# Batched DMA transposes in a fused attention and wave-MLP kernel: q in one long transpose and a tail, batch 2 by TensorE

## The chip, the cores and the metric

The kernel runs on one core of one Trainium2 chip. The metric is the device time of one execution in microseconds; lower is better. Each kernel is executed many times, and the median stands for it. The profile records one further execution on the core: its span runs from the first to the last instruction, and the execution's own time includes what lies around the span.

The engines in the profile are PE (TensorE matmuls), PEld (TensorE weight loads), DVE (VectorE), ACT (ScalarE), POOL (GpSimd) and SP (SyncE, which here issues the DMAs of the main work). A trailing q, as in SPq, names an engine's sequencer.

## The reference

Eight batches of 576 tokens, 8 heads of 64. First a linear attention without softmax, with a norm per head; its output, heads side by side, is x of 576x512 per batch. Then a token mixer with phases and a channel mixer.

```
kv  = k^T v                      per head, 64x64
o   = q kv
x   = o / sqrt(mean(o*o) + 1e-6) * g_norm
theta = x @ w_theta              512x512
y   = w_tok_r @ (x * cos(theta)) + w_tok_i @ (x * sin(theta))      576x576 over tokens
u   = x + y
out = u + max(u @ w_ch, 0)       512x512
```

Inputs and output are float32. Inside, everything but kv is computed with float16 operands.

## The kernel before

Tokens of a batch are cut into four full tiles of 128 and a last one of 64 (`ti` or `j` from 0 to 4, `NF` = 4 full ones, `T` = 64). Heads are handled in four pairs `hp`, so that a pair fills 128 partitions; channels are cut into four chunks `kc`. A batch passes these stages:

- `load` brings q, k and v by head pair (12 transfers of 256 or 288 KB a batch) and the 64 last tokens in the tails kl, vl, ql of 128 KB. `cast_q` casts q on VectorE to float16 in `qcast`, of which there are two, used by even and odd batches.
- q has to lie with channels on partitions. For batches 0 and 1, `by_pair` does that with TensorE: four transposes of 128x128 a pair (`qTps`), copied from PSUM to `qT`, and `turn_q_tail` for the last 64 tokens. For batches 2 to 7, `turn_q` (L502 to L514) issues five DMA transposes from SyncE, one for each token tile, of 128x512 and 64x512, from `qcast` to `qT`.
- `attention` forms k^T v of a pair in PSUM (kv) and copies it to the block-diagonal `kvbd`. `norm` multiplies q with it (raw), squares on ScalarE (sq), sums per head on VectorE (ss), takes the power -1/2 on GpSimd (rt), and scales on VectorE (x).
- `turn_x` transposes x by TensorE (xTps) and scales it by g_norm on ScalarE (xT).
- `phase` forms theta (th), takes it to the range of the sine with pt (ScalarE), f and fa (VectorE), computes both sines on ScalarE (tr), and multiplies by x (z, VectorE).
- `mix` forms y transposed, over six pieces of a batch, and adds x on VectorE (uT).
- `channel` needs u with tokens on partitions: TensorE transposes uT (ups) and ScalarE copies it (u), except for batches 5 and 6 (`U_FROM` = 5), where DMA transposes of 256 columns bring it to `ub`, eight a batch. Then vps = u @ w_ch on TensorE, ot = max(vps, 0) + u on VectorE, and a store by SyncE.

`load_weights` brings w_theta (wst), both mixers (wmix) and w_ch (wcs) in chunks through a ring of 6 staging buffers (`wst` in `SLOTS`); each chunk is cast to float16 by whichever of ScalarE, VectorE or GpSimd the planner picks, which frees its buffer. `mixer_step` transposes the mixers with TensorE to `wT`. `idle_work` offers TensorE filler matmuls named `warm`.

Nothing runs in the order in which it is written here. Each step is added to `Weave` with the engines that could do it, a cost, a due time, what it needs, and the buffers it makes and uses. `Weave.run` goes through a planned time of its own and, for each engine, picks the step that can start soonest and is due first; then it writes the instructions down. The due times come from `DUE`: a first time and a step per item, shifted by `PERIOD` per batch. `MARGIN`, `SLACK`, `URGENT` and `WARM` set how the planner chooses. `in_traced_order` fixes the resulting order on each engine. At run time each engine takes its instructions in exactly this order, so one that waits holds back everything behind it on its engine. This holds for SyncE's DMA queue as well: a DMA whose semaphore is not there yet holds back all later ones, loads and stores alike. The planner itself gives at most 8 DMAs in flight (`LANES`).

```
SLOTS = {
    "kv": 1, "raw": 2, "tp": 2, "th": 1, "mm": 3,
    "k": 6, "v": 6, "q": 6, "ql": 1, "tails": 2, "qc": 2, "qT": 2, "bd": 2, "sq": 2, "ss": 6,
```

`SLOTS` says how many buffers of a kind there are; kv, raw, tp and mm are the eight PSUM banks, and mm serves th, y, vps and warm alike.

Of the kernel before, what the change touches and what calls it, by code (L numbers as in the profile page):

```python
# [18 lines left out]
PERIOD = 25.94  # L19
START = 4.0  # L20
DUE = {
    "load": (-10.17, 8.21),
    "theta": (6.75, 0),
    "mixers": (16.79, 2.63),
    "wch": (26.26, 6.01),
    "wT": (19.93, 1.18),
    ("phase", 0): (10.7, 0),
    ("mix", 0): (28.21, 4.45),
    ("channel", 0): (37.27, 8.33),
    ("phase", 1): (10.01, 3.64),  # L30
    ("mix", 1): (40.08, 5.47),
    ("channel", 1): (54.07, 9.91),
    ("first", 1): (-17.91, 0),
    "first": (-12.95, 0.43),
    "cast": (23.48, 1.17),
    "turn_q": (-8.79, 0),
    "attention": (-4.98, 1.92),
    "norm": (6.64, 1.4),
    "turn": (5.35, 1.03),
    "phase": (19.29, 3.62),  # L40
    "mix": (52.62, 3.55),
    "channel": (67.69, 3.8),
# [5 lines left out]
    "wst": 6, "z0": 2, "z1": 2, "z2": 2, "z3": 2, "z4": 2,  # L48
# [3 lines left out]
U_FROM = 5  # L52
X_FROM = 8
MIX_AFTER = 3
WCH_AFTER = 9


class Weave:
# [8 lines left out]
    SLACK = {"PE": 0.045, "ACT": 0.032, "DVE": 0, "POOL": 0.1, "SP": 0.05}  # L67
    MARGIN = {"PE": 0.282, "ACT": 0.015, "DVE": 0.624, "POOL": 0.1, "SP": 0.0}
    LANES = 8
    BEGIN = {"PE": 1.6, "ACT": 3.2, "DVE": 1.7, "POOL": 2.5, "SP": 0.73}  # L70
    WARM = 69.2
    COLD = 5.0
    URGENT = 2.7
# [20 lines left out]
    def run(self):  # L94
# [92 lines left out]
        assert all(t[0][0] == "warm" for t in ready) and not wanted  # L187
# [19 lines left out]
def kernel(  # L207
# [112 lines left out]
    def idle_work(n):  # L320
        name = f"warm{n}"

        def fn(e):
            t = ps("mm", [P, SH], FP32, name)
            nc.tensor.matmul(
                t[:], kv_bd[1][:, 0, :], kv_bd[1][:, 0:2, :].rearrange("p h c -> p (h c)"),
                start=True, stop=True,
            )

        weave.add(("warm", n), [("PE", 0.11, 0.2, False)], 1e6, fn, makes=[("mm", name)])  # L330

    def load(b, hp):
# [31 lines left out]
        for (i, (kind, src)) in enumerate((("q", q), ("k", k), ("v", v))):  # L364
            full = kind == "q" or b >= QUAD
            weave.add((kind, b, hp), [sp(0.47 if full else 0.42)], due("load", b, hp) + 0.01 * i, part(kind, src),
                      makes=[(kind, f"{kind}{b}_{hp}")], dma=dma(0.85 if b == 0 and hp < 2 else 0.73), load=True)
        if hp == (0 if b else HP - 1):
            for (i, (kind, src)) in enumerate((("kl", k), ("vl", v), ("ql", q))):
                if b < QUAD and kind != "ql":  # L370
                    continue
                weave.add((kind, b), [sp(0.64)], due("load", b, hp) + 0.04 + 0.01 * i,
# [4 lines left out]
                          dma=dma(1.1), load=True)  # L377
# [124 lines left out]
    def turn_q(b):  # L502
        for j in range(NT):
            def fn(e, j=j):
                if j == 0:
                    st["qT", b] = sb("qT", [P, HP, S], FP16, f"qT{b}")
                rows = P if j < NF else T
                nc.sync.dma_start_transpose(
                    out=st["qT", b][:, :, j * P:j * P + rows],
                    in_=qcast[b % 2][:rows, j].rearrange("p h d -> p (h d)"),  # L510
                )
            weave.add(("qT", b, j), [sp(1.3)], due("turn_q", b, j), fn,
                      needs=[("qc", b, hp) for hp in range(HP)] + [("qcl", b)],
                      makes=[] if j else [("qT", f"qT{b}")],  # L514
                      uses=[f"qc{b}"] + ([f"qT{b}"] if j else []),
                      dma=dma(1.05))

    def attention(b, hp):
        def fn(e):
# [3 lines left out]
            if b >= QUAD:  # L523
                for j in range(NT):
                    for r in range(2):
                        nc.tensor.matmul(  # L526
                            kvp[r * D:(r + 1) * D, hp, :],
                            st["k", b, hp][:, r, j, :] if j < NF
                            else st["kl", b][:, 2 * hp + r, :],
                            st["v", b, hp][:, r, j, :] if j < NF  # L530
                            else st["vl", b][:, 2 * hp + r, :],
                            start=(j == 0), stop=(j == NT - 1),
                        )
                return
            for j in range(NS):
                for r in range(2):
                    half = slice(r * PH, (r + 1) * PH)
                    nc.tensor.matmul(  # L538
                        kvp[r * D:(r + 1) * D, hp, :], st["k", b, hp][half, j, :],
                        st["v", b, hp][half, j, :], start=(j == 0), stop=(j == NS - 1),  # L540
                    )
# [19 lines left out]
    def norm(b, ti):  # L561
# [4 lines left out]
        def product(e):  # L566
            t = st[raw] = ps(bank, [P, C], FP32, raw)
            for hp in range(HP):
                qT = st["qT", b][:, hp, :]
                for (rows, cols) in (  # L570
                    ((slice(0, P), slice(ti * P, (ti + 1) * P)),) if ti < NF
                    else ((slice(0, T), slice(SF, S)), (slice(T, P), slice(SF, S)))
                ):
                    nc.tensor.matmul(  # L574
                        t[rows, hp * P:(hp + 1) * P], qT[:, cols], kv_bd[b % 2][:, hp, :],
# [39 lines left out]
        qTs = [("qT", b, i) for i in range(NT)]  # L615
# [14 lines left out]
    def by_pair(b, hp):  # L630

        raw, sq, ss, rt, px, pq = (f"{n}{b}h{hp}" for n in ("raw", "sq", "ss", "rt", "xTps", "qTps"))
        at = due("first", b, hp)
        home = "xT" if b else "uT"
        pair = slice(2 * hp, 2 * hp + 2)
        bank = "mm" if b == 0 and hp > 1 else "raw"
        (qTn, bdn, kvn, xn, xTn) = (f"{n}{b}" for n in ("qT", "bd", "kv", "xp", "xT"))
# [9 lines left out]
        def keep_q0(e):  # L647
            if hp == 0:
                st["qT", b] = sb("qT", [P, HP, S], FP16, qTn)
            t = st["qT", b][:, hp, 0:SF]  # L650
            if e == "ACT":
                nc.scalar.copy(out=t, in_=st[pq][:])
            else:
                nc.vector.tensor_copy(t, st[pq][:])
# [10 lines left out]
        def product(e):  # L665
            t = st[raw] = ps(bank, [P, NF, P], FP32, raw)
            for ti in range(NF):
                nc.tensor.matmul(
                    t[:, ti, :], st["qT", b][:, hp, ti * P:(ti + 1) * P], kv_bd[b % 2][:, hp, :],
# [51 lines left out]
        def keep(e):  # L721
# [6 lines left out]
            else:  # L728
# [5 lines left out]
        weave.add((pq,), [pe(0.25)], at, turn_q0, needs=[("qc", b, hp)], makes=[("tp", pq)],  # L734
                  uses=[f"qc{b}"])
        weave.add(("qT", b, hp), [act(SF), dve(0.35, True)], at, keep_q0, needs=[(pq,)],
                  makes=[] if hp else [("qT", qTn)], uses=[pq] + ([qTn] if hp else []))
# [20 lines left out]
    def turn_q_tail(b):  # L758
# [10 lines left out]
        def keep(e):  # L769
            t = st["qT", b][:, :, SF:S]  # L770
# [5 lines left out]
        at = due("first", b, HP - 1) - 0.1  # L776
# [5 lines left out]
    def turn_x(b, ti):  # L782
# [38 lines left out]
        if b >= X_FROM:  # L821
            weave.add(("xd", b, ti), [sp(1.3)], at, turn_by_dma, needs=[(f"x{b}_{ti}",)],
                      makes=[("xT", f"xT{b}")] if start else [],
                      uses=[f"x{b}_{ti}"] + ([] if start else [f"xT{b}"]), dma=dma(1.05))
# [148 lines left out]
    def channel(b, ti):  # L973
# [49 lines left out]
        def turn_by_dma(kc, half):  # L1023
            def fn(e):
                if not kc and not half:
                    st["ub", b] = sb("ub", [P, NF, C], FP16, f"ub{b}")
                nc.sync.dma_start_transpose(
                    out=st["ub", b][:, 2 * half:2 * half + 2, kc * P:(kc + 1) * P],
                    in_=st["uT", b][:, kc, half * SH:(half + 1) * SH],
# [9 lines left out]
        elif ti % 2 == 0:  # L1039
            for kc in range(NK):  # L1040
                weave.add(("ud", b, kc, ti // 2), [sp(0.8)], at - 2.0, turn_by_dma(kc, ti // 2),
                          needs=[("uT", b, 2 + kc if ti else kc // 2)],
# [72 lines left out]
```

## Time and profile before

| what | value |
|---|---|
| time, median of 11 runs | 230.75 us (227.09 to 233.35) |
| the profiled execution's own time | 231.21 us |
| its span | 229.4 us |
| granted TensorE clock | 1.0 |
| PE, DVE, ACT, POOL busy | 92%, 78%, 68%, 35% of the span |
| HBM read, written | 33.06 MB, 9.44 MB |
| q transposes by DMA | 30, median 3.6 us from issue to landing |
| u transposes by DMA | 16, median 2.3 us |

Busy times are sums over one execution. Matmuls are pipelined, and the end of one is modelled, so a busy TensorE may still hold stops: its rate is read from the starts of matmuls that follow each other. In lists of waits a line reads: engine and line that waited, what ended the wait, then total us, number and the longest. In the chain in order of time a line gives its start, its length and what held the chain then. In a timeline of SyncE a line gives start and length, the latter from the first issue to the end of the last of a merged group; the number after x counts instructions. In a tile's view three numbers with slashes are the shortest, median and longest duration in ns. DMA share is the mean busy share of the core's 16 DMA engines.

The loads are spread over most of the span: the last v of batch 7 lands at 162.0 us. The last matmul starts at about 225 us, and the last store lands at 228.4.

### The profile page before, as it was taken

The page shows a single profiled execution, that of the slowest core. Times are in us where ns is not written, and L with a number is a line of the kernel's source. Part 1 is how long each engine was busy: PE and PEld are TensorE (multiplying, and loading weights), DVE is VectorE, ACT ScalarE, POOL GpSimd, SP SyncE. Part 2 cuts the span into 40 slices and gives each one's busy share as a digit, 9 for nine tenths or more (in the row PEclk, how much of TensorE's full clock was granted, in tenths as well). Part 3 has the DMA queues.
Part 4 walks back from the last instruction along what each step waited for, and adds up shares of the span by engine and source line. Part 5 has one row for each costly group of instructions (what it writes and reads, how often), then busy time and mean ns, then how long its engine had stood idle before and what let it go on. Part 6 is the DMA issues. An engine that isn't in the chain of part 4 may idle for free.

```text
span 229.4 us, 5990 instructions
## 1 busy us (share of the span) xinstructions
PE 211.2 (92%) x2354; PEld 144.6 (63%) x2354; DVE 179.6 (78%) x359; ACT 156.0 (68%) x303; POOL 81.1 (35%) x94
## 2 busy tenths in 40 slices
PE   6779979999977999799988989999999999999992
PEld 4666568874656666575666656567657666657661
DVE  2177798695966699988887879998999898986552
ACT  3378989683990789767867678797788766663031
POOL 6024304660006533560264507532654065500000
PEclk9999999999999999999999999999999999999999
DMA  6999999999759978999699699999532323323414
GB/s 198 376 304 292 281 338 281 239 359 229 143 155 311 296 94 209 352 291 102 201 292 266 150 330 311 248 159 272 147 88 83 83 57 116 106 57 92 163 46 160
DMA packets 62399, 47.47 MB, mean 207 GB/s; under 512 B 32548, under 2 KB 54052, under 8 KB 62372
## 3 DMA queue, kind: packets, MB, share of 16 engines
q1 hardware_dynamic: 62368, 47.11, 77.9%
q8 instruction: 18, 0.29, 0.6%
q14 instruction: 9, 0.07, 0.1%
q10 hardware_dynamic: 4, 0.00, 0.0%
HBM read 33.06 MB, written 9.44 MB: 185 GB/s over the span
## 4 chain that ended last, share of the span: by engine, by line
PE 56%; DMA 25%; DVE 9%; SPq 3%; ACT 2%; issue 2%; POOL 1%; DVEq 0%; POOLq 0%
PE y L940 23%; PE vps L998 10%; DMA q<-in_q_dram 8%; PE th L844 7%; DMA k<-in_k_dram 6%; DMA v<-in_v_dram 5%; DMA wst<-in_moe_w_theta_dram 3%; PE kv L526 3%; PE raw L574 3%; DVE f L860 2%; PE xTps L791 2%; PE kv L538 2%; DMA wmix<-in_moe_w_tok_r_dram 2%; PE ups L989 2%; SPq L339 1%
## 5 line engine op out<-in xcount | busy, mean ns | idle before, releaser
L940 PE MATMUL y<-wT,z 128*128 128x320 f16 (+1 forms) x576 | 77.9, 286 | 0.8 <-DVE f L860 0.8
L940 PEld LDWEIGHTS <-z 128*128 128x128 f16 x576 | 54.5, 98 | 16.9 <-issue 1.6
L596 POOL TENSOR_TENSOR rt<-ss,mhalf 128x8 f32<-128x8 f32 x31 | 53.3, 1720 | 2.6
L592 POOL TENSOR_SCALAR ss<-ss 128x8 f32<-128x8 f32 x31 | 9.6, 308 | 85.4 <-DVE ss L585 84.7
L998 PE MATMUL vps<-wch,uT 128*128 128x512 f16 (+1 forms) x192 | 37.2, 344 | 0.0
L951 DVE SCALAR_TENSOR_TENSOR uT<-y,gcol,xT 128x320 f16<-128x320 f32 (+1 forms) x48 | 29.3, 611 | 6.5 <-PE y L940 6.3
L844 PE MATMUL th<-wth,xT 128*128 128x512 f16 x128 | 32.3, 380 | 0.7 <-DVE f L860 0.5
L856 ACT ACTIVATE pt<-th,magic_t 128x512 f32<-128x512 f32 (+1 forms) x40 | 25.5, 641 | 8.6 <-PE th L844 5.5
L800 ACT ACTIVATE xT<-xTps,gcol 128x512 f16<-128x512 f16 (+1 forms) x32 | 20.1, 632 | 13.5 <-PE xTps L791 12.9
L860 DVE SCALAR_TENSOR_TENSOR f<-pt,th 128x512 f32<-128x512 f32 (+1 forms) x40 | 24.9, 627 | 4.1 <-ACT pt L856 4.0
L879 ACT ACTIVATE tr<-f 128x512 f16<-128x512 f32 x32 | 19.9, 628 | 11.1 <-DVE f L860 11.0
L484 DVE CAST qcast<-q 128x512 f16<-128x512 f32 x32 | 13.7, 432 | 16.0 <-DMA q<-in_q_dram 15.0
L1005 ACT COPY u<-ups 128x512 f16<-128x512 f16 (+1 forms) x32 | 16.4, 526 | 13.8 <-PE ups L989 13.6
L879 ACT ACTIVATE tr<-fa,pio_t 128x512 f16<-128x512 f32 x32 | 22.9, 720 | 2.0 <-DVE fa L867 1.7
L608 DVE TENSOR_TENSOR x<-raw,rt 128x512 f16<-128x512 f32 x32 | 21.9, 684 | 1.5 <-POOL rt L596 1.1
L585 DVE TENSOR_REDUCE ss<-sq 128x8 f32<-128x512 f32 x32 | 21.5, 677 | 1.9 <-ACT sq L581 1.8
L1009 DVE SCALAR_TENSOR_TENSOR ot<-vps,u 128x512 f32<-128x512 f32 (+1 forms) x32 | 19.5, 616 | 3.2 <-PE vps L998 2.0
L897 DVE TENSOR_TENSOR z<-x,tr 128x1024 f16<-128x1024 f16 (+1 forms) x32 | 19.7, 616 | 1.5 <-ACT tr L887 1.4
L998 PEld LDWEIGHTS <-uT 128*128 128x128 f16 (+1 forms) x192 | 14.4, 102 | 9.8 <-issue 0.8
L581 ACT ACTIVATE sq<-raw 128x512 f32<-128x512 f32 x32 | 18.8, 592 | 0.2 <-PE raw L574 0.2
L844 PEld LDWEIGHTS <-xT 128*128 128x128 f16 x128 | 11.5, 98 | 11.6 <-issue 0.9
L526 PE MATMUL kv<-v,k 128*64 128x64 f32 x384 | 16.0, 226 | 2.0 <-DMA v<-in_v_dram 2.0
(96 smaller groups left out, 270.7 us busy)
## 6 DMA issues: line engine op xcount, KB each, us to landing
q<-in_q_dram SPq DMA_DIRECT2D x32, 256.0 KB, 5.7
out_dram<-ot SPq DMA_DIRECT2D x32, 256.0 KB, 2.7
k<-in_k_dram SPq DMA_DIRECT2D x24, 256.0 KB, 5.9
v<-in_v_dram SPq DMA_DIRECT2D x24, 256.0 KB, 5.9
k<-in_k_dram SPq DMA_DIRECT2D x8, 288.0 KB, 5.6
v<-in_v_dram SPq DMA_DIRECT2D x8, 288.0 KB, 6.1
wmix<-in_moe_w_tok_r_dram SPq DMA_DIRECT2D x4, 288.0 KB, 5.6
wmix<-in_moe_w_tok_i_dram SPq DMA_DIRECT2D x4, 288.0 KB, 4.3
```

Source lines behind the costliest of these rows:

```text
L526: nc.tensor.matmul(kvp[r * D:(r + 1) * D, hp, :], st["k", b, hp][:, r, j, :] if j < NF else st["kl", b][:, 2 * hp + r, :], st["v", b, hp][ ...
L585: nc.vector.reduce_sum(out=t[:], in_=st[sq][:].rearrange("p (h e) -> p h e", h=H), axis=mybir.AxisListType.X,)
L596: nc.gpsimd.tensor_tensor(out=r[:], in0=t[:], in1=mhalf[:], op=ALU.pow)
L608: nc.vector.tensor_tensor(out=t[:].rearrange("p (h e) -> p h e", h=H), in0=st[raw][:].rearrange("p (h e) -> p h e", h=H), in1=st[rt][:].un ...
L800: nc.scalar.activation(out=st["xT", b][:, :, cols], in_=st[px][:, :, 0:cols.stop - cols.start], func=AFT.Copy, scale=gcol[:],)
L844: nc.tensor.matmul(t[:], xT[:, kc, :], wth[:, kc, :], start=(kc == 0), stop=(kc == NK - 1),)
L856: nc.scalar.activation(out=t[:], in_=st[th][:], func=AFT.Identity, bias=magic_t[:])
L860: nc.vector.scalar_tensor_tensor(out=t[:], in0=st[pt][:], scalar=MAGIC, in1=st[th][:], op0=ALU.subtract, op1=ALU.subtract,)
L879: nc.scalar.activation(out=t[:, which, :], in_=src[:], func=AFT.Sin, scale=-RAD, bias=0.0 if bias is None else bias[:],)
L940: nc.tensor.matmul(st[y][:, c, :], z[:, kc * P:(kc + 1) * P], wT[m][:, cols], start=(c == 0 and m == 0) if open_sums else m == 0, stop=m = ...
L951: nc.vector.scalar_tensor_tensor(out=st["uT", b][:, chunks, cols], in0=st[y][:], scalar=gcol[:], in1=st["xT", b][:, chunks, cols], op0=ALU ...
L998: nc.tensor.matmul(t[half], uT(kc), wch[:, kc, r * n:(r + 1) * n], start=(kc == 0), stop=(kc == NK - 1),)
```

## The change

- q of batches 3 to 7: `turn_q` issues two DMA transposes instead of five: one of 128x2048 (all four full token tiles) and one of 64x512. `qT` gets the layout token tile, head pair, token, so that the long transpose writes one stretch of it.
- q of batch 2: turned by TensorE like that of batches 0 and 1, by the new function `turn_q_pair` (taken out of `by_pair`) and `turn_q_tail`. `Q_DMA` = 3 says from which batch on DMA does it.
- u of batches 4, 5 and 6 by DMA (`U_FROM` = 4), in four transposes of 512 columns a batch instead of eight of 256; each now needs both pieces of a channel chunk.
- 8 staging buffers for weights; w_ch is loaded after load group 7 instead of 9 (`WCH_AFTER`).
- All due times and the planner's parameters are new, some planned DMA costs too. A filler now needs the filler before it. The order of instructions on every engine therefore differs throughout.

```diff
-PERIOD = 25.94
+PERIOD = 25.97
 DUE = {
-    "load": (-10.17, 8.21),
+    "load": (-5.25, 8.21),
-    "turn_q": (-8.79, 0),
-    "attention": (-4.98, 1.92),
-    "norm": (6.64, 1.4),
-    "turn": (5.35, 1.03),
-    "phase": (19.29, 3.62),
-    "mix": (52.62, 3.55),
-    "channel": (67.69, 3.8),
+    "turn_q": (-14.96, 0.38),
+    "attention": (-4.52, 2.35),
+    "norm": (6.64, 2.8),
+    "turn": (-0.22, 0.91),
+    "phase": (18.27, 3.54),
+    "mix": (51.38, 3.12),
+    "channel": (67.54, 4.04),
...
-    "wst": 6, "z0": 2, "z1": 2, "z2": 2, "z3": 2, "z4": 2,
+    "wst": 8, "z0": 2, "z1": 2, "z2": 2, "z3": 2, "z4": 2,
...
-U_FROM = 5
+Q_DMA = 3
+U_FROM = 4
-WCH_AFTER = 9
+WCH_AFTER = 7
...
     def turn_q(b):
-        for j in range(NT):
-            def fn(e, j=j):
-                if j == 0:
-                    st["qT", b] = sb("qT", [P, HP, S], FP16, f"qT{b}")
-                rows = P if j < NF else T
-                nc.sync.dma_start_transpose(
-                    out=st["qT", b][:, :, j * P:j * P + rows],
-                    in_=qcast[b % 2][:rows, j].rearrange("p h d -> p (h d)"),
-                )
-            weave.add(("qT", b, j), [sp(1.3)], due("turn_q", b, j), fn,
-                      needs=[("qc", b, hp) for hp in range(HP)] + [("qcl", b)],
...
+        def main(e):
+            t = st["qT", b] = sb("qT", [P, NT, HP, P], FP16, f"qT{b}")
+            nc.sync.dma_start_transpose(
+                out=t[:, 0:NF].rearrange("p j h t -> p (j h) t"),
+                in_=qcast[b % 2][:, 0:NF].rearrange("p j h d -> p (j h d)"),
+            )
+
+        def tail(e):
+            nc.sync.dma_start_transpose(
+                out=st["qT", b][:, NF, :, 0:T],
+                in_=qcast[b % 2][0:T, NF].rearrange("p h d -> p (h d)"),
+            )
+
+        cast = [("qc", b, hp) for hp in range(HP)]
+        weave.add(("qT", b, 0), [sp(1.4)], due("turn_q", b, 0), main, needs=cast,
+                  makes=[("qT", f"qT{b}")], uses=[f"qc{b}"], dma=dma(3.0))
+        weave.add(("qT", b, 1), [sp(1.3)], due("turn_q", b, 1), tail, needs=[("qcl", b), ("qT", b, 0)],
+                  uses=[f"qc{b}", f"qT{b}"], dma=dma(0.8))
...
-                qT = st["qT", b][:, hp, :]
+                qT = st["qT", b][:, ti, hp, 0:P if ti < NF else T]
...
-        def turn_by_dma(kc, half):
+        def turn_by_dma(kc):
             def fn(e):
-                if not kc and not half:
+                if not kc:
                     st["ub", b] = sb("ub", [P, NF, C], FP16, f"ub{b}")
                 nc.sync.dma_start_transpose(
-                    out=st["ub", b][:, 2 * half:2 * half + 2, kc * P:(kc + 1) * P],
-                    in_=st["uT", b][:, kc, half * SH:(half + 1) * SH],
+                    out=st["ub", b][:, :, kc * P:(kc + 1) * P], in_=st["uT", b][:, kc, 0:SF]
                 )
...
+                if b < Q_DMA:
+                    turn_q_pair(b, hp, due("turn_q", b, hp))
-        if b < 2:
+        if b < Q_DMA:
             turn_q_tail(b)
-        if b > 1:
+        else:
             turn_q(b)
```

The new function, as called for batch 2:

```
    def turn_q_pair(b, hp, at):
        pq, qTn = f"qTps{b}h{hp}", f"qT{b}"
        pair = slice(2 * hp, 2 * hp + 2)

        def turn_q0(e):
            t = st[pq] = ps("tp", [P, SF], FP16, pq)
...
        def keep_q0(e):
            if hp == 0:
                st["qT", b] = sb("qT", [P, NT, HP, P], FP16, qTn)
            t = st["qT", b][:, 0:NF, hp, :]
            src = st[pq][:].rearrange("p (j t) -> p j t", j=NF)
...
        weave.add((pq,), [pe(0.25)], at, turn_q0, needs=[("qc", b, hp)], makes=[("tp", pq)],
                  uses=[f"qc{b}"])
        weave.add(("qT", b, hp), [act(SF), dve(0.35, True)], at, keep_q0, needs=[(pq,)],
                  makes=[] if hp else [("qT", qTn)], uses=[pq] + ([qTn] if hp else []))
```

## Prediction

> **What bounds the kernel now.** I read the page first (busy shares, slices, chain), then the waits of TensorE and VectorE between 50 and 140 us, the chain in order of time, SyncE's own timeline and the table of ten-microsecond windows.
>
> ```profile
> PE 211.2 (92%) x2354; PEld 144.6 (63%) x2354; DVE 179.6 (78%) x359; ACT 156.0 (68%) x303; POOL 81.1 (35%) x94
> PE 56%; DMA 25%; DVE 9%; SPq 3%; ACT 2%; issue 2%; POOL 1%; DVEq 0%; POOLq 0%
> ```
>
> TensorE looks full, but that share overstates it. The chain shows `0.86 PE th L844 x4`, four matmuls of 512 columns, so a column costs 0.42 ns. I priced all matmuls of the program's order like that (an fp32 kv group at its traced 0.73 us): 193 us of real work plus 6.3 us of `warm` filler in 229.4. For each matmul group I then took its start less the real work ahead of it in program order. This lag is 14.4 us at the first theta product (22.6 us), 18.5 at the first y0 (35.4), 20.1 at th1_0 (53.2), 31.6 at th4_4 (136.7) and 32.7 at the end. So TensorE loses 11.5 us between 53 and 137 us and only 1.1 after it. A gain must come from the middle. Who holds it there:
>
> ```profile
> PE xTps L791 <- DVE x L608: 2.8, 4, 0.9
> PE kv L526 <- DMA v<-in_v_dram: 2.0, 3, 1.1
> PE ups L989 <- ACT u L1005: 1.0, 1, 1.0
> PE y L940 <- DVE f L860: 0.8, 1, 0.8
> ...
> DVE qcast L484 <- DMA q<-in_q_dram: 8.8, 9, 2.0
> DVE qcast L490 <- DMA ql<-in_q_dram: 1.5, 1, 1.5
> ```
>
> The first four lines are TensorE's waits, the last two VectorE's, same window. TensorE waits for v directly, and for x and f because VectorE, which takes its work in order, stands in front of a cast whose q has not landed. Late loads are the cause of both. The chain in order of time agrees:
>
> ```profile
> 68.02 6.21 DMA v<-in_v_dram
> 74.25 5.09 DMA q<-in_q_dram
> ...
> 88.23 4.79 DMA k<-in_k_dram
> 93.03 0.87 SPq L339
> 93.95 6.26 DMA q<-in_q_dram
> ```
>
> Why the loads are late is in SyncE's timeline and the q transposes' rows:
>
> ```profile
> 77.06 7.41 SPq L508 DMA_TRANSPOSE qT<-qcast  x5
> 84.57 1.47 SPq L1016 DMA_DIRECT2D out_dram<-ot  x1
> ...
> 87.56 0.63 SPq L339 DMA_DIRECT2D q<-in_q_dram  x1
> L508 SPq DMA_TRANSPOSE qT<-qcast x30: 1218/1262/3916, 54.1 to 166.3; - x30
> L1027 SPq DMA_TRANSPOSE ub<-uT x16: 1168/1196/2431, 177.6 to 210.1; - x16
> ```
>
> One queue issues everything. From 77.06 to 87.56 us no q, k or v load is issued: five transposes hold the queue 7.4 us. The landings tell the price: I summed a service time per transfer in queue order (256 KB 0.735 us, 288 KB 0.76, a 128x512 transpose 0.475, from spacings of landings in busy stretches) and compared with the landings. They are late by 11.3 us at v2_3 (lands 55.1), 17.8 at v3_1 (72.1), 23.5 at v4_1 (93.9), 28.6 at v5_1 (115.0) and 34.1 at v6_1 (136.2). Each burst of five costs the DMA stream 5.1 to 6.5 us in which it moves too little.
>
> ```profile
> 80.00:90.00 10.00, 9.76 (x97) 6.04 (x96) 10.00 (x19) 8.80 (x17) 3.20 (x3) 1.00 0.76 128
> 170.00:180.00 10.00, 10.00 (x114) 6.70 (x112) 8.86 (x16) 8.84 (x16) 4.03 (x4) 1.00 0.17 59
> ```
>
> After the length stand PE, PEld, DVE, ACT, POOL and the clock; last is DMA share and GB/s. At 80 us, mid-load, the stream has fallen to 128 GB/s; at 170 the loads are over, and with the same kinds of compute work TensorE never stops. That is how the middle could run.
>
> **What the Trainium skill says.** *Trainium Kernel Development and Optimization*, Performance Expectations: matmul busy time is a bad metric since matmuls are pipelined. It agrees: 92% busy, 84% (193 of 229.4) by start-to-start work. *DMA: Bandwidth & Descriptors*, Anatomy of one DMA: DMA engines do not wait on semaphores, the issuing sequencer does, before dispatch. So a transpose waiting for its cast stops all behind it, as the 7.41 us line shows (5 x 1.26 is 6.3). The same page, Rules for kernel authors, puts a DMA transpose with a non-contiguous middle dimension at 261 GB/s: 512 KB of q would take 2.0 us, an estimate; four traced landings at 0.475 give 1.9. Merging saves no data time.
>
> **The change, part by part.** Durations are from the profiled execution: 231.21 us around a span of 229.4; it lies 0.46 above the median of 230.75.
>
> *q of batches 3 to 7.* Five issues become a main one (2048 columns) and a tail, placed apart in the queue with loads between. No row shows a 2048-column issue. Low: 256 to 512 columns rise from 1.196 to 1.262 us, so six more steps of 0.066 give 1.66. High: four times 1.262, 5.05. I take 1.7, since doubling the columns cost 5%. The tail stays at 1.26, so the queue is held 3.0 us per batch, not 6.3. The wait for all four casts stays; behind it stand vl, ql and the next q, k, v. The price of waiting is covered if loads run ahead: with the bursts gone, v3_1 has no transpose ahead of it and can land near 63 instead of 72. The tiles raw b_0 read only the first 512 columns before and now wait for all 2048; main lands about 1.9 + 2.3 us after issue (2.3 is the fastest ub landing), and between the earliest issue that its casts (in batch 7 the u transposes ahead of it) allow and raw b_0 the new order has over 10 us of matmul work in every batch: free.
>
> *q of batch 2.* Its burst (54.1 to 64.8 us in SyncE's queue) goes, with about 2304 packets. TensorE gets 16 transposes at 0.055 and a tail: +0.96 us of work, on the path. Four copies of 0.58 and one of 0.37 go to ScalarE and VectorE at about 48 to 57 us, where ScalarE is 59 to 75% busy: hidden.
>
> *u of 4 to 6.* Batch 4 loses 16 transposes (-0.85 us TensorE) and four 0.58 us copies (ScalarE, hidden). Its four DMA issues and the four longer ones for 5 and 6 stand behind the last load in the queue, where the share has fallen to 0.17 to 0.58: hidden, and vps does not read them. TensorE net: +0.1.
>
> *Weight buffers.* wmix_0_2 is issued 3.4 us after wmix_0_1, waiting for a theta cast; two more buffers lift that. It could bring v1_0 (lands 30.09, its kv starts 30.23) up to 2 us forward, but ScalarE is 87 to 92% busy from 20 to 40 us and gets about 1.1 us more casts. Between +1 and -2; I take -0.5. The loads of w_ch move ahead of q2_1, k2_1 and v2_1, which land 2.8 us later (4 x 0.69), near 49 us; the new order needs them in kv2_1 behind th1_3, near 56: hidden. So are ql0 behind five mixer loads, since raw0_4 moves behind th0_2, and two w_ch casts of 0.62 on GpSimd, 16 to 61% busy there.
>
> *The waits that go.* TensorE's stops above 0.35 us between 53 and 137 us, start to start, sum to 9.6. Ten (0.66, 0.64, 1.06, 0.37, 1.30, 0.62, 0.65, 0.73, 0.99 and 0.94) stand behind a late v or vl, or behind a VectorE operation that came after a waiting cast: 8.0 us. The other 1.65 (ups0_4 behind ScalarE, then a filler) I halve: -0.8.
>
> *What is late next.* The new order is tighter. From raw b_0 to its x transposes the old order had 7.2, 7.7, 7.7 and 5.9 us of other matmul work in batches 3 to 6; the new has 4.8, 5.9, 5.9 and 5.8. The fastest traced chains (square, sum, power, scale) take 5.65 and 5.90 us, in batches 7 and 6. Batch 3 then stops about 1.0, and by the same comparison (third tiles: traced 5.54, new 5.4, 5.5 and 5.0; x transposes to th4_0: traced 1.5, new 1.1) 1.2 more: +2.2. This runs from 0 to 12 (below).
>
> Sum: 231.2 - 8.0 - 0.8 - 0.5 + 0.1 + 2.2 = 224.2; on the median's footing 223.8.
>
> **Rivals.** *Issue time grows with columns (17%).* A main then takes 5.05 us and the bursts of 3 to 7 stay; only batch 2's goes. For: the trace has no issue above 512 columns. Against: the 5% step. Gone are 1.7 us at v3_1 and x2_0, half of the other 6.3, and 0.5 at the start; the rest as above: 231.2 - 1.7 - 3.1 - 0.5 + 0.1 + 2.2 = 228.2, 227.7 on the median.
>
> *All stops go and the tight order costs nothing (13%).* 231.2 - 9.6 - 1.5 + 0.1 = 220.2, or 219.7. The start gives 1.5 here. For: after 137 us the lag grows 1.1 in 88 us. Against: batch 3's 4.8 is below any traced chain.
>
> *The tight chain takes over (15%; slower).* Place: TensorE's queue in front of xTps b_0, batches 3 to 6. In the old trace three of these chains took 8.5, 8.6 and 9.1 us. If they are that long by themselves (8.7), the stops are 4 x 8.7 - 22.4 = 12.4 us against 9.2 saved: 234.4, or 233.9. It decides from 7.9 us up. For: VectorE is at 80 to 100% there, so x queues behind other work. Against: in those three TensorE had 7.2 to 7.7 us to do anyway and VectorE waited for q within them; in the new order three to six VectorE operations stand between sum and scale, against five to seven.
>
> **How the numbers follow.** Forecast 55% (221 to 227). About 1%, 2.3 us, is what a measurement can tell from no change. Faster: 55 and 13 and half of 17, less a little: 75%. Same: the other half and some edges, 11%. Slower: 14%. The range goes from 219.5 (everything goes) to 231.0; the slower rival is left out.
>
> **What would show it.** Right: main issues under 2 us, loads of batch 4 landing 8 us or more earlier, the casts' waits for q after 50 us under 2 us, the lag near 24 to 26 at the end, and chain DMA share well below 25%. Wrong: mains of 5 us; waits of xTps for x above 5 us; or the lag at th1_0 already over 21, a loss at the start.

## The result, and the profile after

The changed kernel takes 226.5 us (median of 12 runs, 226.12 to 227.47); the kernel before takes 231.15 us in the runs since (median of 47, 227.09 to 234.06). The medians stand at 0.980. The ratio of the compared runs is 0.987, 95% interval 0.9845 to 0.9894; it is nearer to one because runs more than 1.5% above the fastest of their kernel are left out, and the kernel before spreads by 3%, the changed one by 0.6%. The forecast was 223.8. The profiled execution took 226.45 us around a span of 224.7, 4.8 less than the one of before.

The page's busy times and its chain:

```profile
PE 213.9 (95%) x2375; PEld 147.3 (66%) x2375; DVE 179.9 (80%) x359; ACT 155.1 (69%) x302; POOL 83.1 (37%) x96
PE 60%; DVE 17%; POOL 11%; ACT 4%; issue 2%; DMA 2%; SPq 1%; DVEq 0%
```

DMA's share of the chain went from 25% to 2%. What TensorE and VectorE wait for between 50 and 140 us (total us, times, longest), TensorE's list whole and VectorE's longest:

```profile
PE xTps L792 <- DVE x L603: 0.9, 3, 0.4
PE th L850 <- ACT xT L801: 0.7, 1, 0.7
...
DVE x L603 <- POOL rt L591: 2.3, 4, 0.8
```

No matmul waits for v there, and no cast for q (8.8 us before). The window at 80 us and SyncE's rows for the q transposes (shortest, median, longest ns; main, then tail):

```profile
80.00:90.00 10.00, 10.00 (x130) 6.53 (x126) 9.27 (x19) 8.99 (x18) 2.69 (x3) 1.00 1.01 261
...
L506 SPq DMA_TRANSPOSE qT<-qcast x5: 1932/3036/4023, 75.6 to 159.9; - x5
L512 SPq DMA_TRANSPOSE qT<-qcast x5: 1192/1237/1312, 83.1 to 165.0; - x5
```

In this window the stream moves 261 GB/s where it moved 128. So the waits of the middle went as forecast; what took them away is a question for e2 and e3 below. Now the lag, formed as in the prediction: the start of a matmul group less the real work ahead of it in TensorE's order, fillers not counted as work. In these names the first number is the batch and the second the head pair or token tile: kv1_0 is k^T v of pair 0 of batch 1, th4_4 is theta of the last token tile of batch 4.

| lag at | before | after | forecast for the stretch that ends here | measured |
|---|---|---|---|---|
| th1_0 (53.2, 54.8 us) | 20.1 | 23.3 | -0.5 | +3.2 |
| th4_4 (136.7, 135.5 us) | 31.6 | 26.4 | -8.0 - 0.8 + 2.2 = -6.6 | -8.4 |
| last vps | 32.7 | 27.8 | 0 | +0.3 |

With the 0.1 us more of work that is -4.8. Against this trace of the kernel before, the middle gave more than forecast. The start, where half a microsecond of gain was booked, lost 3.2, and nearly all of it lies ahead of kv1_0, the first matmul group on v of batch 1. Its lag is 16.6 before and 20.0 after. TensorE's timeline up to it, before:

```profile
28.24 0.41 PE L463 MATMUL wTps<-ident,wnat 128*128 128x128 f16 x4
28.58 0.22 PE L463 MATMUL wTps<-ident,wnatl 64*128 64x64 f16 x1
29.07 0.38 PE L642 MATMUL qTps1h<-ident,qcast 128*128 128x128 f16 x4 [0.27 <-DVE wT L473]
30.23 1.26 PE L538 MATMUL kv<-v,k 64*64 64x64 f32 x36 [0.78 <-DMA v<-in_v_dram]
```

and after:

```profile
27.16 2.56 PE L326 MATMUL warm<-kvbd 128*128 128x256 f16 x8
29.56 0.38 PE L464 MATMUL wTps<-ident,wnat 128*128 128x128 f16 x4
29.88 0.22 PE L464 MATMUL wTps<-ident,wnatl 64*128 64x64 f16 x1
30.03 0.28 PE L326 MATMUL warm<-kvbd 128*128 128x256 f16 x1
30.15 0.39 PE L464 MATMUL wTps<-ident,wnat 128*128 128x128 f16 x4
30.47 0.22 PE L464 MATMUL wTps<-ident,wnatl 64*128 64x64 f16 x1
30.62 1.91 PE L326 MATMUL warm<-kvbd 128*128 128x256 f16 x6
32.37 0.38 PE L632 MATMUL qTps1h<-ident,qcast 128*128 128x128 f16 x4
32.68 1.26 PE L536 MATMUL kv<-v,k 64*64 64x64 f32 x36
```

Before, kv1_0 waits for its v and starts 0.14 us after v1_0 landed (30.09). After, v1_0 lands at 29.05, a microsecond earlier, as the larger ring of weight buffers was to bring, but kv1_0 starts 3.6 us later than that, because fifteen fillers stand ahead of it. Eight of them take from 27.16 to 29.56, 0.30 us each on average. They count as busy, so the list of waits shows nothing of it; the busy share of TensorE even rose, from 92% to 95%.

### The profile page after: what moved, and what is told of

The parts are those of the page before. It is cut to its first block, busy times and chain, and to the rows that moved or that the text cites. A ratio compares the mean times of both kernels' runs of the same rounds, so it can differ in the third digit from the quotient of the medians.

```text
span 224.7 us, 6007 instructions
## 1 busy us (share of the span) xinstructions
PE 213.9 (95%) x2375; PEld 147.3 (66%) x2375; DVE 179.9 (80%) x359; ACT 155.1 (69%) x302; POOL 83.1 (37%) x96
## 4 chain that ended last, share of the span: by engine, by line
PE 60%; DVE 17%; POOL 11%; ACT 4%; issue 2%; DMA 2%; SPq 1%; DVEq 0%
PE y L941 19%; PE th L845 9%; PE vps L999 9%; POOL rt L591 9%; PE kv L536 6%; PE warm L326 5%; DVE x L603 4%; DVE ss L580 3%; DMA v<-in_v_dram 2%; DVE f L861 2%; PE xTps L792 2%; DVE z L898 2%; PE raw L569 2%; POOL ss L587 2%; DVE ot L1010 2%
## 5 line engine op out<-in xcount | busy, mean ns | idle before, releaser
L941 PE MATMUL y<-wT,z 128*128 128x320 f16 (+1 forms) x576 | 77.0, 286 | 0.0
L941 PEld LDWEIGHTS <-z 128*128 128x128 f16 x576 | 54.6, 98 | 16.7 <-issue 1.2
L591 POOL TENSOR_TENSOR rt<-ss,mhalf 128x8 f32<-128x8 f32 x31 | 54.9, 1772 | 2.6
L801 ACT ACTIVATE xT<-xTps,gcol 128x512 f16<-128x512 f16 (+1 forms) x32 | 20.1, 630 | 14.3 <-PE xTps L792 14.0
L857 ACT ACTIVATE pt<-th,magic_t 128x512 f32<-128x512 f32 (+1 forms) x40 | 25.6, 643 | 4.2 <-PE th L845 3.9
L536 PE MATMUL kv<-v,k 128*64 128x64 f32 (+1 forms) x672 | 26.1, 224 | 0.9 <-DMA v<-in_v_dram 0.9
L536 PEld LDWEIGHTS kv<-v,k 128*64 128x64 f32 (+1 forms) x672 | 22.5, 137 | 6.1 <-issue 3.5
L1006 ACT COPY u<-ups 128x512 f16<-128x512 f16 (+1 forms) x28 | 14.3, 519 | 15.5 <-PE ups L990 15.4
L580 DVE TENSOR_REDUCE ss<-sq 128x8 f32<-128x512 f32 x32 | 21.5, 680 | 3.3 <-ACT sq L576 3.1
L880 ACT ACTIVATE tr<-f 128x512 f16<-128x512 f32 x32 | 20.1, 628 | 5.7 <-DVE f L861 5.5
L898 DVE TENSOR_TENSOR z<-x,tr 128x1024 f16<-128x1024 f16 (+1 forms) x32 | 19.7, 616 | 1.8 <-ACT tr L888 1.2
L1010 DVE SCALAR_TENSOR_TENSOR ot<-vps,u 128x512 f32<-128x512 f32 (+1 forms) x28 | 17.0, 609 | 3.3 <-PE vps L999 2.3
L326 PE MATMUL warm<-kvbd 128*128 128x256 f16 x76 | 16.1, 304 | 2.9 <-DVE root_d L292 1.5
```

Of the source, the lines that this page charges most:

```text
L326: nc.tensor.matmul(t[:], kv_bd[1][:, 0, :], kv_bd[1][:, 0:2, :].rearrange("p h c -> p (h c)"), start=True, stop=True,)
L536: nc.tensor.matmul(kvp[r * D:(r + 1) * D, hp, :], kt, vt, start=(j == 0), stop=(j == (NT if b >= QUAD else NS) - 1),)
L580: nc.vector.reduce_sum(out=t[:], in_=st[sq][:].rearrange("p (h e) -> p h e", h=H), axis=mybir.AxisListType.X,)
L591: nc.gpsimd.tensor_tensor(out=r[:], in0=t[:], in1=mhalf[:], op=ALU.pow)
L857: nc.scalar.activation(out=t[:], in_=st[th][:], func=AFT.Identity, bias=magic_t[:])
L880: nc.scalar.activation(out=t[:, which, :], in_=src[:], func=AFT.Sin, scale=-RAD, bias=0.0 if bias is None else bias[:],)
```

## The experiments

The theory after this reading: the fillers cost the start, and without them the change is worth what the middle gained. The rivals: the lost time comes from something else in the new order (the mixers, w_ch moved forward), or the middle's gain is not the merged transpose's. All lags in one table; medians are of 4 runs or more except for single executions, marked 1.

| kernel | us | lag kv1_0 | th1_0 | th4_4 | last vps |
|---|---|---|---|---|---|
| before | 231.15 | 16.6 | 20.1 | 31.6 | 32.7 |
| after | 226.5 | 20.0 | 23.3 | 26.4 | 27.8 |
| e1: after, no late fillers | 222.14 | 16.7 | 18.6 | 21.8 | 23.2 |
| e5: after, fillers of a run on one tile | 224.13 | 17.7 | 20.7 | 23.9 | 25.3 |
| e11: after, hardly any filler | 223.08 | 16.1 | 18.1 | 21.2 | 23.4 |
| e10: before, no late fillers | 231.45 (1) | 15.6 | 20.5 | 30.1 | 32.9 |
| e2: after, long transpose cut in four | 227.71 | 19.9 | 23.1 | 26.3 | 28.4 |
| e3: before, transposes merged | 225.17 | 16.4 | 20.6 | 25.6 | 26.6 |
| e4: before, one transpose of five | 222.82 | 17.5 | 23.2 | 26.2 | 27.0 |
| e6: e1 with six weight buffers | 222.32 | 17.8 | 19.7 | 22.8 | 24.2 |
| e7: e1, u of batch 4 by TensorE | 224.42 | 17.7 | 19.8 | 23.0 | 25.3 |
| e8: e1, q of batch 2 by DMA | 222.79 | 16.8 | 18.8 | 23.1 | 24.5 |

Two executions of one order can differ: in a kernel whose work is that of e1 up to its end (e9 below) the lag at th1_0 was 20.1 instead of 18.6, and it was 1.4 later already at the first theta product. Lag differences of that size say little by themselves.

**e1: the fillers left out.** From warm57 on (19 of them), in place:

```diff
         def fn(e):
+            if n >= 57:
+                return
             t = ps("mm", [P, SH], FP32, name)
```

> The changed kernel with every filler matmul behind the first theta tiles left out (warm57 and later, 19 of them); each other instruction stands where it stood. Theory A (the start lost what the prediction promised: with three of the mm banks' slots held by theta tiles, fillers follow each other at 0.33 us instead of 0.11 and hold kv1_0, ready at 29.0, until 32.7): the lag at th1_0 falls from 23.3 to about 20, kv1_0 starts within 1 us of the landing of v1_0, time 226.5 - 3.4 = 223 us. Rival B (the start is bound by ScalarE and VectorE, the fillers only fill): the lag at y0_0 stays near 21.9 and the time within 1 us of 226.5. Rival C (the fillers keep TensorE at speed): transposes and matmuls behind 27 us get slower and the time rises.

222.14 us (221.69 to 223.72), ratio to before 0.9745 (0.9611 to 0.9879), 4.4 below after. kv1_0 starts at 29.37 instead of 32.68, and the lag stays 4.6 to 4.7 lower from th1_0 to the end. From th1_0 to th4_4 it grows by 3.2, as after's grows by 3.1: the start was the whole of what was missing.

**e5: as many fillers, but without a tile of their own.**

```diff
-            t = ps("mm", [P, SH], FP32, name)
+            if n < 57 or n in (57, 65, 66, 72, 75):
+                st["warm"] = ps("mm", [P, SH], FP32, name)
+            t = st["warm"]
```

> The changed kernel with all its fillers in the same places; only, from warm57 on, the fillers of one run (57 to 64, 66 to 71 and so on) write one PSUM tile instead of a new tile each, so that none has to wait for the one before it. Theory A (the start is late because a filler tile waits for its predecessor's bank, 0.33 us each instead of 0.11): the lag at kv1_0 falls from 20.0 to about 17.5, at th1_0 from 23.3 to about 20, and the time to 223 us (222 to 224.5). Rival B (the number of matmuls, or their work, is what costs, wherever they write): nothing changes, 226.5 us, lag at th1_0 23.

224.13 us (223.86 to 224.63), 2.4 below after and 2.0 above e1. Its timeline of TensorE:

```profile
27.41 1.05 PE L328 MATMUL warm<-kvbd 128*128 128x256 f16 x8
28.29 0.39 PE L466 MATMUL wTps<-ident,wnat 128*128 128x128 f16 x4
...
29.35 0.83 PE L328 MATMUL warm<-kvbd 128*128 128x256 f16 x6
30.02 0.39 PE L634 MATMUL qTps1h<-ident,qcast 128*128 128x128 f16 x4
30.33 1.26 PE L538 MATMUL kv<-v,k 64*64 64x64 f32 x36
```

The same eight matmuls now take 0.88 us (27.41 to 28.29) instead of 2.40. So the loss has two halves. One is the fillers' own work, 19 times 0.11, 2.1 us. The other, 2.4, is that a filler with a new tile waits until the matmul before it has come to its end. The trace shows this wait: in a run of the changed kernel each filler from the second on carries a wait for the semaphore that TensorE's own matmuls count up, and follows the one before after 0.33 us (27.50, 27.83, 28.15), its length being 0.27; in e5 the fillers from the second to the last of a run carry no wait and follow after 0.11. One bank by itself does not slow matmuls that follow each other: here they write the same one. That the theta products held the other two banks of mm at that time is read from the program's order and was not tried by itself. The rival "it is their number" is half right.

**e10 and e11: are fillers dear everywhere?** e10 leaves out those of the kernel before from warm48 on (11), e11 those of the changed kernel from warm22 on (another 35), both by the edit of e1 with another number.

> The kernel before without its fillers from warm48 on (11 of them, 1.2 us of work). Theory A (fillers cost the changed kernel its start because there are 19 in a row of heads, one bank free; in the kernel before they stand in stops): kv1_0 at 30.2, the lag at th1_0 within 0.8 us of 20.1, and the time within 1 us of before. Rival B (the fillers cost before as much, so they are no loss of the change): lag at th1_0 2 us or more lower.

> The changed kernel without fillers from warm22 on (another 35 go, which stand between the first raw tiles and th0_0). Rival B for what fillers do (they keep TensorE's clock up while it has little to do): clock records below 1.0 between 15 and 30 us, th0 at half speed, 2 to 5 us more than 222.1. Theory A (they only fill, and what they wait in front of comes late): 221.5 to 222.3, th0_0 at 21.5 to 22.

e10: 231.45 us, lag 20.5 at th1_0. kv1_0 starts 1.0 earlier and nothing is left of it at th1_0: in the kernel before, the fillers stood in stops. This is one execution and the scatter is 1.5, so a loss of about 1 us could hide in it, but not one of 4.4: the loss belongs to the new order. e11: 223.08 us (222.05 to 223.51), no gain over e1. th0_0 came 1.7 us earlier (20.31 against 22.03), but the windows from 18 to 24 us show why that is not kept:

```profile
18.00:20.00 2.00, 0.09 (x2) 0.10 (x3) 1.49 (x4) 1.59 (x4) 0.79 (x2) 0.81 1.14 194
20.00:22.00 2.00, 2.00 (x8) 0.74 (x9) 0.00 (x0) 1.64 (x3) 0.48 (x2) 0.50 1.04 307
22.00:24.00 2.00, 2.00 (x12) 0.82 (x11) 1.43 (x4) 1.81 (x5) 0.49 (x2) 0.84 1.08 320
```

TensorE worked 0.09 us of two (first number after the length of the window), the granted clock (third from the end) fell to 0.50, and theta ran at half speed. So fillers do have a use, and the early ones, which stand in a real stop, earn about what they cost. The late ones do not earn 4.4 us. Of the five traces without them (e1 and e6 to e9) one, e7, shows the clock falling to 0.50 at 30 us, and its lag at th1_0 was 19.8 against 18.6 in e1.

**e2, e3, e4: is the middle's gain the merged transpose's?** e2 cuts the main transpose of the changed kernel into four of 512 columns, one behind the other (first diff). e3 keeps the order of before and only merges: `j == 0` issues the main, `j == NF` the tail, the rest nothing. e4 keeps the order of before and issues the first of five only (all tiles then read its columns, so most of q is left out).

```diff
-            nc.sync.dma_start_transpose(
-                out=t[:, 0:NF].rearrange("p j h t -> p (j h) t"),
-                in_=qcast[b % 2][:, 0:NF].rearrange("p j h d -> p (j h d)"),
-            )
+            for j in range(NF):
+                nc.sync.dma_start_transpose(
+                    out=t[:, j], in_=qcast[b % 2][:, j].rearrange("p h d -> p (h d)"),
+                )
```

and e3, then e4:

```diff
-                    st["qT", b] = sb("qT", [P, HP, S], FP16, f"qT{b}")
...
+                    t = st["qT", b] = sb("qT", [P, NT, HP, P], FP16, f"qT{b}")
+                    nc.sync.dma_start_transpose(
+                        out=t[:, 0:NF].rearrange("p j h t -> p (j h) t"),
+                        in_=qcast[b % 2][:, 0:NF].rearrange("p j h d -> p (j h d)"),
+                    )
+                if j == NF:
+                    nc.sync.dma_start_transpose(
+                        out=st["qT", b][:, NF, :, 0:T],
+                        in_=qcast[b % 2][0:T, NF].rearrange("p h d -> p (h d)"),
+                    )
```

```diff
-                if j == 0:
-                    st["qT", b] = sb("qT", [P, HP, S], FP16, f"qT{b}")
+                if j:
+                    return
+                st["qT", b] = sb("qT", [P, HP, S], FP16, f"qT{b}")
```

> The changed kernel with each q transpose of 2048 columns cut back into four of 512, issued one after the other at the same place; all else stands. Theory A (it was the place and the distance of the loads, not the merging, that took the waits away; the new order has slack): the queue is held about 5 us instead of 3 per batch, loads land up to 2 us later, the time stays within 1 us of 226.5. Rival B (the shorter hold of the queue is what pays): 5 batches of 2 us more, waits for q come back, 229 us or more.

> The kernel before in its own order, with only the q transposes of batches 2 to 7 merged: one of 2048 columns at the place of the first and the tail at the place of the fifth, and qT laid out as in the change. Theory A (the burst's hold of the queue makes the loads late): SyncE is held about 4.3 us instead of 6.3 per burst (the changed kernel's main took 3.0 us in its trace), six bursts, loads 2 us earlier each, the lag between th1_0 and th4_4 grows by 8 to 10 us instead of 11.5, time 1 to 3 us below before. Rival B (place and order decide): within 1 us of before.

> The kernel before in its own order with only the first of the five q transposes of each of the batches 2 to 7 issued; the raw products of all token tiles read its 128 columns, so that q of the other tiles is left out. Theory A (the bursts make the loads late, and late loads make the stops in the middle): 5 us less of the queue per burst and 1792 packets less of DMA, the casts' waits for q between 50 and 140 us fall from 8.8 to under 3, the lag between th1_0 and th4_4 grows by under 5 instead of 11.5, time 5 to 8 us below before. Rival B (the order of VectorE and ScalarE makes the stops): within 2 us of before.

e2: 227.71 us (226.65 to 229.07), ratio 0.9934 (0.99 to 0.9968): 1.2 slower than after. Its row of issues and TensorE's waits from 50 to 140 us, whole:

```profile
L507 SPq DMA_TRANSPOSE qT<-qcast x20: 1223/1264/2731, 75.4 to 165.2; - x20
...
PE xTps L792 <- DVE x L603: 0.9, 3, 0.4
PE th L850 <- ACT xT L801: 0.8, 1, 0.8
```

These waits are those of the changed kernel, and from th1_0 to th4_4 the lag grows by 3.2 as after's grows by 3.1. Yet the q transposes of e2 hold SyncE for 36.3 us in all, summed over their issues in the trace, or 7.3 a batch; the kernel before has 45.3 in six batches, 7.5 each, and the changed one 21.5 in five, 4.3 each. So in the new order the middle is as good without the long transpose: its gain in the changed kernel is not owed to the shorter hold, and the second rival is right there. The 1.2 comes behind th4_4, where the lag ends at 28.4 instead of 27.8 and TensorE has a stop of 0.54 us at 162.4 that after lacks.

e3: 225.17 us, ratio 0.9875 (0.9762 to 0.9987): by merging alone, in the old order, 6.0 below before by the medians and 2.9 by the ratio, and 1.3 below the whole change. e4: 222.82 us, ratio 0.9777 (0.9644 to 0.991); its profiled execution alone took 225.54, with the clock at half for 6.8 us from 30.5 us on, hence its lag of 23.2 at th1_0. In the old order the transposes therefore hold back about 8 us by the medians (5 by the ratio), of which merging frees 6 (3). The new order and the merging are two remedies for the same waits: either takes most of them away, and what they save does not add up. Which part of the new order does it (loads ahead of the main, main and tail apart, q of batch 2 on TensorE) was not separated: e2 undoes the merging and e8 the part of batch 2, each alone and at 1.2 us or less, and both together were not tried.

Rows of e3:

```profile
L507 SPq DMA_TRANSPOSE qT<-qcast x6: 2305/4985/5783, 53.9 to 155.3; - x6
L512 SPq DMA_TRANSPOSE qT<-qcast x6: 1191/1242/1405, 60.3 to 157.6; - x6
...
DVE qcast L484 <- DMA q<-in_q_dram: 2.9, 5, 0.9
```

Here a main holds the queue for 5.0 us (median), with its tail as long as five issues of 1.26. But the median of single issues hides the long ones. Summed over the issues in the traces, the six bursts of before hold SyncE for 45.3 us (42.7 in e0, its second trace), the mains and tails of e3 for 35.7: 1.2 to 1.6 us less a batch. The casts wait 2.9 us for q instead of 8.8, and the last v of batch 7 lands at 156.1 instead of 162.0: 5.9 us over six batches, one microsecond each, which fits that sum.

**e9: the price of the issue.** e1 with two transposes each of 512, 1024 and 2048 columns behind its last store, on data long there.

```diff
     weave.run()
+    for i in range(2):
+        nc.sync.dma_start_transpose(out=st["qT", 6 + i][:, NF], in_=src[i][:, 0:512])
...
+        nc.sync.dma_start_transpose(
+            out=st["qT", 6 + i][:, 0:NF].rearrange("p j h t -> p (j h) t"), in_=src[i])
```

> The changed kernel without fillers from warm57 on, with six extra DMA transposes behind the last store, when all that they read is long there: two of 512 columns, two of 1024, two of 2048. It prices the issue alone. The prediction's low figure (the issue hardly grows with the columns): 1.26, 1.4 and 1.7 us. Its high one (it grows with them): 1.26, 2.5 and 5.0. Between them: about 3 us for 2048, as the median in the changed kernel, would say that the 3.0 there is the issue and not waiting.

```profile
L1090 SPq DMA_TRANSPOSE qT<-qcast x2: 1219/1220/1221, 219.2 to 220.5; - x2
...
L1092 SPq DMA_TRANSPOSE ub<-qcast x2: 1299/1310/1322, 221.7 to 223.1; - x2
...
L1095 SPq DMA_TRANSPOSE qT<-qcast x2: 2204/2296/2387, 224.5 to 226.9; - x2
```

1.22, 1.31 and 2.30 us. Neither line of the prediction holds: up to 1024 columns the issue hardly grows, then it does. The remaining 0.7 of the 3.0 in the changed kernel, and 2.7 of the 5.0 in e3, are not there in a quiet queue; that the other transfers in flight cause them was not tried by itself.

**e6, e7, e8: the other parts, without the fillers over them.** e6 sets the staging ring back to six. e7 turns u of batch 4 by TensorE (16 transposes and four copies by ScalarE into `ub`). e8 turns q of batch 2 by a main transpose and a tail.

```diff
-                    [P, S], FP32, tag="wst", bufs=SLOTS["wst"], name="_".join(map(str, name))
+                    [P, S], FP32, tag="wst", bufs=6, name="_".join(map(str, name))
```

```diff
+            if b == 4 and ti < NF:
+                pt4 = ps("tp", [P, n], FP16, f"u4ps{ti}")
...
+                nc.scalar.copy(out=st["ub", b][:, ti, :], in_=pt4[:])
```

```diff
+            if b == 2:
+                if hp == HP - 1:
+                    nc.sync.dma_start_transpose(
+                        out=st["qT", b][:, 0:NF].rearrange("p j h t -> p (j h) t"),
+                        in_=qcast[b % 2][:, 0:NF].rearrange("p j h d -> p (j h d)"),
+                    )
...
```

> The changed kernel without fillers from warm57 on (222.1 us), its ring of weight staging buffers cut back from eight to six. Theory A (the buffers do what they are for, the fillers hid it): v1_0 lands about 1 us later, near 30 us, kv1_0 starts 1 us later, 223.0 us (222.6 to 223.6). Rival B (the buffers are worth nothing, because the casts on ScalarE or the chain from theta set the start): 222.1, within 0.5.

> The changed kernel without fillers from warm57 on (222.1 us), u of batch 4 turned by TensorE and copied by ScalarE instead of by DMA. Theory A (TensorE's order is the bound, what it gets extra is paid in full): 16 transposes of 0.055 us, 0.9 us, so 223.0. Rival B (the transposes lie in stops that are there anyway, or the four DMA transposes cost the queue as much): 222.1, or up to 1 us less.

> The changed kernel without fillers from warm57 on (222.1 us), q of batch 2 turned by one DMA transpose of 2048 columns and a tail, as q of 3 to 7 are, instead of by TensorE. Theory A (work taken from TensorE counts in full, and a merged transpose costs the loads little): 0.96 us less, 221.2. Rival B (the main transpose waits for its casts at 50 to 60 us with the loads of batch 3 behind it, so that v3 comes late and TensorE stops): 1 to 4 us more, 223 to 226, with waits of TensorE or VectorE for loads of batch 3 in the trace.

e6: 222.32 us (221.69 to 222.83), no difference that can be told. v1_0 lands at 29.66 instead of 29.06, so the two buffers bring at most 0.6 of its microsecond; the 1.1 of its higher lag is there at the first theta product already and is within the scatter named above. The rival holds.

e7: 224.42 us (224.05 to 228.84), 2.3 more. Of that 0.85 is the transposes' work, as priced; another 0.86 is a stop ahead of the third group of them, which waits until ScalarE has copied xT out of the PSUM bank that the group needs. In the profiled execution the dip of the clock is in it too; two others, at a mean clock of 0.999 and above, took 224.05 and 224.07. Turning u of 4 by DMA is worth about 1.9 against transposes at this place, more than the work it takes off TensorE; a place without that stop was not tried.

e8: 222.79 us, no gain. TensorE had 0.96 us less to do, but the main of batch 2 is held long, v3_1 lands at 67.2 instead of 61.0, and VectorE and TensorE wait in turn. Its row and its waits from 50 to 100 us:

```profile
L646 SPq DMA_TRANSPOSE qT<-qcast x1: 4096/4096/4096, 54.6 to 54.6; - x1
...
PE xTps L811 <- DVE x L605: 1.2, 2, 0.9
...
DVE qcast L487 <- DMA q<-in_q_dram: 1.6, 2, 1.0
```

So q of batch 2 by TensorE is a trade at par.

**e0: the kernel before, once more.**

> The kernel before once more, for a second trace of it. It says how far its middle moves from one execution to the next: lag at kv1_0 16.6 and at th1_0 20 in both; if the growth from th1_0 to th4_4 (11.5 in the first trace) is 9 to 14, the part of the gain that is measured against one execution is uncertain by that much.

229.02 us. th1_0 starts at 53.1 as in the first trace, th4_4 at 134.4 instead of 136.7. Between the two the lag thus grows by 9.3; by 9.6 in e10, by 11.5 in the trace the prediction used. The place of the loss is the same, its size varies by 2 us. That is a part of the spread of the kernel before, which is 7 us over all its runs, and the 8.4 gained in the middle is 6.2 to 6.5 against the other two executions.

## Why the prediction was wrong

The direction was right and the size was not: 4.7 us by the medians, 3.0 by the ratio, instead of 7.

- **What bounds it: right.** Late loads behind the bursts of transposes (e3, e4); they left the chain (25% to 2%), the casts' waits for q went from 8.8 to none, and v4_1 lands 7.6 us earlier (86.2), just short of the 8 named.
- **The shorter hold as the remedy: not what did it here.** The prediction let the waits go because the queue is held 3.0 us per batch and not 6.3, and its slower-issue rival brought half of them back with mains of 5 us. In e2 the queue is held 7.3 per batch and the middle gains as much: the new order takes the waits away by itself. Both holds were also mis-sized, being worked out from the median issue: measured over all issues they are 7.5 before and 4.3 after. And the 1.1 us by which the line of 7.41 exceeds five issues is no wait for a cast, as the prediction reads it: the last of the four casts ended at 76.02, the wait for it ahead of the burst takes 0.03 us, and the first of the five issues itself takes 2.18.
- **The stops that go, and the tight order (-8.0 - 0.8 + 2.2): right in kind, measured -8.4.** Against the two other traces of before's order (e0 and e10) it is -6.2 and -6.5, so how near the sum of -6.6 comes is in part luck of the trace. The new stops of TensorE above 0.35 us after 57 us sum to 3.1, none over 0.92. Batch 3 was to stop about 1.0 at its x transposes and stops 0.44. The slower rival, chains of 8.7 us, did not show: xTps waits 0.9 in all between 50 and 140 us.
- **The main's issue (1.7): mis-sized.** 2.3 alone and 3.0 in the kernel, and the main lands 6.0 us (median) after its issue, not about 4.2. It did little harm, since in the new order even four issues (e2) cost only 1.2 more. (The 261 GB/s that the prediction takes for the data time stands in the section "Latency and other measured facts" of *DMA: Bandwidth & Descriptors*, not in the one named.)
- **The start (-0.5): the step that failed.** It asked what eight buffers do for v1_0 and ScalarE's casts, and set TensorE's net work at +0.1, real work alone. The fillers of the new order were counted nowhere, though 19 of them stand in it ahead of the late wT, qTps and kv groups. I had taken fillers for what fills stops, which is true of the kernel before, as far as one execution shows (e10), and not of the new order. They measured 4.4 us (e1): 2.0 of work, 2.4 of waiting for each other's tiles (e5). Without them the lag at th1_0 is 18.6 in e1 and 20.1 in e9, which has the same order, against 20.1 before; so whether the booked half microsecond was there is not shown. The time without them is 222.1, below the forecast. "The lag at th1_0 over 21, a loss at the start" was named as the sign that would prove the forecast wrong; it is 23.3.
- **Weight buffers: nothing measurable in the time (e6)**, though v1_0 lands 0.6 us earlier with them.
- **The rivals.** Issue time in proportion to columns is out by e9 (2.3 us, not 5). "All stops go" (219.7) lies 2.4 below what the change does without its fillers (222.1), the forecast (223.8) 1.7 above it. The slower rival is answered above.

The fastest here is e1: 222.1 us, 4.4 below the changed kernel.

## What to carry to other kernels

Price every instruction of the new order, fillers too: a busy engine hides them from every list of waits, and only start to start against the work behind them shows what they hold back. Fillers belong in stops that are there at run time; where a planner places them by its own clock, look at what stands behind each one and whether that was ready. When two parts of a change touch different stretches, take the lag at a point between them, since a gain in one can hide the loss in the other. And undo each part alone before you credit it: here a shorter hold of the queue and a better order cured the same waits, and either was nearly enough.

## What the runs showed of the hardware

- A filler of 256 columns that needs a new PSUM tile while none is free follows the one before at 0.33 us (after), its length in the profile being 0.27; writing the same tile as its predecessor, it follows at 0.11 (e5).
- The issue of a DMA transpose of 128 partitions on SyncE, queue otherwise quiet (e9): 1.22 us for 512 columns, 1.31 for 1024, 2.30 for 2048; its landing follows 2.4, 3.4 and 4.5 us after the issue. Among the other work 2048 columns took 1.9 (after) to 5.8 (e3).
- The clock. The Trainium skill, *TensorE: Matmul & The Clock Gate*, Part 1, names two states of the clock gate, full and half, and advises under "Why this matters for your kernels" to keep idle gaps under about 3 us. The half state agrees (0.50 in e4, e7 and e11). The gap alone does not account for e7, where the clock fell with no idle time near that. The windows of e7:

```profile
28.00:30.00 2.00, 1.26 (x27) 1.04 (x26) 1.49 (x6) 1.99 (x4) 0.00 (x0) 0.97 1.09 280
30.00:32.00 2.00, 2.00 (x31) 1.60 (x27) 1.11 (x2) 1.17 (x4) 0.00 (x0) 0.50 1.07 376
32.00:34.00 2.00, 2.00 (x23) 1.37 (x22) 1.66 (x4) 1.94 (x7) 0.00 (x0) 0.67 1.08 373
```

TensorE was busy 1.26 us of two before the fall, its longest idle time there was 0.66 us, and the clock then stayed at half for about 3.4 us (0.1 + 2 + 1.3, from the three windows). With the same order e1 kept 1.00. In the 3.4 us before the fall TensorE ran nothing but transposes, and from 29.40 on a kv group; whether transposes count less for the clock than other matmuls no run here tries.
